# Talking-heads attention and a squared-ReLU FFN: head weights spread by TensorE, later loads, and a last tile in three parts

## The chip, the cores and the metric

The kernel runs on one core of one Trainium2 chip. The metric is the device time of one execution in microseconds. Engines are named as in the profile: PE is TensorE (PEld its weight loads), DVE is VectorE, ACT is ScalarE, POOL is GpSimd, and SP is the engine that issues most DMAs.

## The reference

Eight batches, twelve heads, 448 positions, head dimension 64. Two 12x12 matrices mix the heads, one before and one after the softmax. The result, 3584 rows of 768, goes through a feed-forward network of width 2048.

```python
scores = scale * np.matmul(q, k.transpose(0, 1, 3, 2))       # scale = 1/8
scores = np.einsum('bhij,hg->bgij', scores, w_pre)
scores = scores - np.max(scores, axis=-1, keepdims=True)
attn = np.exp(scores)
attn = attn / (np.sum(attn, axis=-1, keepdims=True) + 1e-09)
attn = np.einsum('bhij,hg->bgij', attn, w_post)
attn_out = np.matmul(attn, v)
x = attn_out.transpose(0, 2, 1, 3).reshape(B * S, H * D)
h = np.maximum(x @ w_in, 0.0)
out = h * h @ w_out
```

All inputs and the output are float32; the matmuls run in bf16.

## The kernel before

**Chunks.** Attention is worked in chunks of ten positions times twelve heads, which are 120 partitions; a batch has 45 chunks, and the run has 360. A chunk `n` goes through a fixed chain. PE mixes the heads of its scores with `wmix` (L775), DVE takes the extreme of each row into `mn` (L786), ACT takes the exponential into `es` with its row sum (L789), DVE takes the reciprocal `rc` (L795), POOL multiplies the head-mixing matrix `wback` by `rc` into `wq` (L798), PE multiplies `es` with `wq` (L805), and DVE or ACT copies that into `atb`. A group of chunks is then multiplied with v (L850) into `xt`, the input of the network.

**Scores.** Scores of 128 positions and one head are computed as 128x448 (L653), copied to `snat` by DVE or ACT, and laid out anew as chunks `sch` by a DMA on SP (L681, a relayout). k and q are transposed before that: in batches 0 and 1 on PE (L509; the last 64 positions of q, the tails, by L549), from batch 2 on by copies `kn<-ks` and `qn<-qs` on POOL or DVE (L584) and a transposing DMA on SP.

**The direct chunks.** In batch 0 the chunks `C0[1] <= c < C0[2]` do not wait for a relayout. For them q is multiplied beforehand with the entries of `w_pre`, on DVE (`f_prep`, L764, into `osb`, used as scratch), and PE forms the mixed scores by six matmuls of 448 columns (L781). The entries stand in `wfan`, which lies in `qn`'s memory and which two DVE operations make from `wall` (L435), a copy of `w_pre` on all partitions. Chunks that are not direct use `wmix` and `wback`, which are made from `wpre_rep`, `wpost_rep` and masks; the direct ones use `wback_far`, made from `wpost_far`.

**The weights of the heads.** Four DMAs on SP bring them, each with a broadcast: `wall` (128 lines of 576 bytes), `wpost_far`, `wpre_rep` and `wpost_rep` (120 lines of 48 bytes each).

**The first loads.** POOL issues k in three pieces (`ks`), q's first 128 positions (in `kn`'s memory), the tails (`qt`) and the rest of q (`qs`), then v and the six pieces of `w_in`. Loads of the next batch are issued on POOL by `load_ahead`, once for heads 0 to 5 and once for heads 6 to 11.

**The network.** Units of 128 or 256 positions: L907 gives `h` (six matmuls per 128 features), DVE or ACT applies the ReLU into `hr` (L921, L925), POOL squares it (L928), and L944 multiplies with `w2` into banks of 384 columns, two per 128 rows. DVE or ACT copies a bank into `osb`, and SP stores it (L968), as 120 rows and 8 rows.

**The order.** A planner (`Planner`) decides the order on every engine when the kernel is built. Each `add` names an engine (or several, with a cost for each), a cost in ns, a priority and what it depends on; the planner plays the run through with these costs and writes down which engine took what when. On the chip each engine then works its list in order. `MOST` limits the banks of each use, `AHEAD` says by how many chunks a relayout goes ahead of its chunk, `gate(n)` holds a load until `wq` of chunk `n`. Where the plan has PE idle early on, it puts in matmuls on zeros (`still`, L1161). The planner's own costs for the first loads and for the preparation on DVE are these:

```python
    set_up = add("DVE", 5300, -100, lambda: None)
...
        at_ += 1.1 if at_ < 2 else 0.75
...
    started = add("POOL", int(1000 * at_) + 700, -100, lambda: None)
```

Of the kernel before, what the change touches and what calls it, by code (L numbers as in the profile page):

```python
# [24 lines left out]
CI = 10  # L25
# [273 lines left out]
def kernel(  # L299
# [124 lines left out]
    def near_back():  # L424
# [4 lines left out]

    smask_far = sb.tile([KC, CI], F32, name="smask_far")  # L430
    nc.vector.tensor_reduce(
        out=smask_far[:, :], in_=ident[0:KC, 0:KC].rearrange("p (h s) -> p s h", h=H), axis=AX.X, op=ALU.add,
    )
    for x in range(2):
        nc.vector.tensor_scalar(  # L435
            out=wfan[64 * x:64 * x + 64],
            in0=wall[64 * x:64 * x + 64, :].rearrange("p (c x g) -> p c x g", x=2, g=H)[:, :, x, :].unsqueeze(3).to_broadcast([D, NPAIR, H, CI]),
            scalar1=-SCALE, scalar2=1.0, op0=ALU.mult, op1=ALU.mult,
        )
    wback_far = sb.tile([KC, H, CI], F32, name="wback_far")  # L440
    nc.gpsimd.tensor_tensor(
        out=wback_far[:, :, :], in0=wpost_far[:, :].unsqueeze(2).to_broadcast([KC, H, CI]),
        in1=smask_far[:, :].unsqueeze(1).to_broadcast([KC, H, CI]), op=ALU.mult,
    )
    qw = [
# [10 lines left out]

    backed = []
    pl = Planner()
# [3 lines left out]
    slots = {}  # L462

    def keep(key, fn):
        def go(*got):
            for key_, slot in zip(key if isinstance(key, list) else [key], got):
                slots[key_] = slot
            fn(*got)
        return go

# [264 lines left out]
    def chunk(b, c):  # L735
# [13 lines left out]
        if far:  # L749
# [4 lines left out]
            for lo, hi, first, x, s0, step, w in (  # L754
                ([(64 * x_, 64 * x_ + 64, 0, zt, P - 8 + x_, 2, 2) for x_ in range(2)] if cc == 0 else []) +
                [(0, P, PIECE * i_, qz[i_], CI * (cc - 1) if cc else P_ROWS - 8, 1, CI if cc else 8) for i_ in range(2)]
            ):
                size = PIECE if lo < hi - 64 else NPAIR
                late = [ready[0, first + y][1][1] for y in range(PIECE)] if size < NPAIR else [ready_tail[0, 0], ready_tail[0, PIECE]]

                def f_prep(eng="DVE", lo=lo, hi=hi, first=first, size=size, x=x, s0=s0, step=step, w=w):
                    o = 2 if w == 8 else 0
                    src_ = x[lo:hi, 0, :, s0:s0 + w] if size < NPAIR else x[lo:hi, :, s0:s0 + step * (w - 1) + 1:step]
                    (nc.vector if eng == "DVE" else nc.gpsimd).tensor_tensor(  # L764
                        out=qw[j][lo:hi, first:first + size, :].rearrange("p c (g s) -> p c g s", g=H)[:, :, :, o:o + w],
                        in0=src_.unsqueeze(2).to_broadcast([hi - lo, size, H, w]),
                        in1=wfan[lo:hi, first:first + size, :, 0:w], op=ALU.mult,
                    )
# [121 lines left out]
    def unit(pair, ui):  # L890
# [47 lines left out]
        for mt in range(w // 128):  # L938
            for nt in range(2):
                key = ("f", ix, "o", mt, nt)  # L940
                for f0 in range(0, FT, 4):
                    def mms(slot, f0=f0, mt=mt, nt=nt):
                        for ft in range(f0, f0 + 4):
                            nc.tensor.matmul(  # L944
                                slot[:, 0:384], lhsT=h2_[:, ft, mt * 128:(mt + 1) * 128],
                                rhs=w2[:, ft, nt * 384:(nt + 1) * 384],
                                start=(ft == 0), stop=(ft == FT - 1),
                            )
                    if f0 == 0:
                        prev = add("PE", 652, fill + 20 + 4 * mt + 2 * nt, keep(key, mms),  # L950
                                   [prev] + sq_op[ix][0:4 // nf] + w2_in[0:1 if ix < SOON else 4], lat=0, bank=key)
                    else:
                        prev = add("PE", 652, FILL, lambda key=key, mms=mms: mms(slots[key]), [prev, w2_in[f0 // 4]] + sq_op[ix][0:(f0 + 4) // nf], lat=0)
# [7 lines left out]
                ev = add({"DVE": 480, "ACT": 440}, 0, 0, evac, [end, st_op.get(si - 2)] + ([m_op[n_] for n_ in direct] if si < 2 else []), lat=100, frees=key)  # L961
                whole = not (z == W2B and mt == 1 and pair == B // 2 - 1)
                evs = evs + [ev] if nt == 1 and whole else [ev]
                if nt == 1 or not whole:
                    done = []
                    for rows, dst, o in pieces(pair, a + mt * 128, None if whole else nt):
                        def store(dst=dst, o=o, rows=rows, si=si, e0=0 if whole else nt * 384, e1=384 if not whole and nt == 0 else DMODEL):
                            nc.sync.dma_start(out=dst, in_=osb[si % 2][o:o + rows, e0:e1])  # L968
                        done.append(add("SP", 510 if rows <= CI else 930, FILL, store, evs))
                    st_op[si] = pl.moved("DMA", 8, 140, 130, 0, done, 1500)  # L970
# [6 lines left out]
    def pieces(pair, pos, part=None):  # L977
        e0, e1 = (0, DMODEL) if part is None else (part * 384, part * 384 + 384)
        got = []
# [25 lines left out]
    def gate(step):  # L1005
        return [wq_op[step]] if step in wq_op else []
# [3 lines left out]

    at_, tails0 = 1.3, []
    for what, x in LOADS0:
        if what == "k":
            k_in[0, x] = first(at_, 28, 48)
        elif what == "q":
            q_in[0, x] = first(at_, 32, 30)
        elif what == "a":
            q_in[0, "a"] = first(at_, 48, 30)
        else:
            tails0.append(first(at_, 24, 24))  # L1020
# [181 lines left out]
```

## Time and profile before

| | |
|---|---|
| median of 3 runs | 585.29 us (584.46 to 587.61) |
| profiled execution | 585.32 us |
| its span | 583.5 us |
| PE busy | 569.2 us (98%), 5813 matmuls |
| DVE busy | 510.9 us (88%) |
| ACT busy | 443.2 us (76%) |
| POOL busy | 321.7 us (55%) |
| granted PE clock | 1.00 |

The span runs from the first to the last instruction that the profile holds. A busy time counts an engine's instructions from start to end; matmuls overlap each other, so PE busy is not PE at its peak. DMA shares are of 16 DMA engines; q0 is the queue that POOL feeds, q1 the one that SP feeds.

### The profile page before, as it was taken

The numbers are of one execution on the slowest core, as the hardware profiler recorded it, in microseconds if no ns is written. First come the engines' busy times: TensorE is split into PE (matmuls) and PEld (weight loads), VectorE is DVE, ScalarE is ACT, GpSimd is POOL, SyncE is SP. The second block draws the span as 40 slices with busy tenths as digits, with TensorE's granted clock in tenths as the row PEclk, the third lists the DMA queues.
The fourth block names the chain that finished last, engine by engine and source line by source line (L and its number), as shares of the span: only waits on it lengthen the run. The fifth ranks groups of instructions, "written<-read, shape, count | busy, mean of one in ns | idle before, by whom it ended". The sixth has DMA issues, their size and how long they took to land.

```text
span 583.5 us, 16716 instructions
## 1 busy us (share of the span) xinstructions
PE 569.2 (98%) x5813; PEld 407.5 (70%) x5813; DVE 510.9 (88%) x1136; ACT 443.2 (76%) x1179; POOL 321.7 (55%) x591
## 2 busy tenths in 40 slices
PE   8999899999999999999999999999999999999996
PEld 5558566777677678667677677767758676767783
DVE  4899998999998999998899998988899998989441
ACT  2688988888797787887887888888788888887200
POOL 7366347646575248735667257734667344635340
PEclk9999999999999999999999999999999999999999
DMA  9999959973797449954596749964397646322021
GB/s 120 213 159 210 185 122 164 205 152 100 143 209 155 125 120 153 188 130 122 102 196 160 163 116 139 197 144 119 95 197 167 155 123 121 116 77 76 2 55 54
DMA packets 132993, 80.98 MB, mean 139 GB/s; under 512 B 60484, under 2 KB 127916, under 8 KB 132908
## 3 DMA queue, kind: packets, MB, share of 16 engines
q1 hardware_dynamic: 85340, 57.11, 38.9%
q0 software_dynamic: 47568, 22.81, 30.7%
q8 instruction: 45, 0.74, 0.5%
q14 instruction: 40, 0.33, 0.2%
HBM read 45.70 MB, written 11.01 MB: 97 GB/s over the span
## 4 chain that ended last, share of the span: by engine, by line
PE 88%; DVE 6%; DMA 3%; issue 1%; ACT 1%; POOL 1%; DVEq 0%; POOLq 0%; ACTq 0%
PE bank L944 25%; PE bank L907 24%; PE bank L805 13%; PE bank L775 11%; PE bank L850 6%; PE bank L653 6%; PE bank L781 2%; DVE mn L786 2%; DMA sch<-snat 2%; DMA ks<-in_k_dram 1%; DVE atb L453 1%; DVE snat L453 1%; PE bank L509 1%; ACT es L789 0%; DVE hr L921 0%
## 5 line engine op out<-in xcount | busy, mean ns | idle before, releaser
L789 ACT ACTIVATE es<-bank,mn 120x448 bf16<-120x448 f32 x360 | 228.7, 641 | 48.4 <-DVE mn L786 44.3
L786 DVE TENSOR_REDUCE mn<-bank 120x1 f32<-120x448 f32 x360 | 209.8, 611 | 4.9 <-PE bank L781 2.9
L798 POOL TENSOR_SCALAR wq<-wback,rc 120x120 bf16<-120x120 f32 (+1 forms) x347 | 122.5, 365 | 157.6 <-DVE rc L795 85.1
L944 PE MATMUL bank<-w,h 128*128 128x384 bf16 x896 | 173.3, 325 | 0.0
L907 PE MATMUL bank<-xt,w 128*128 128x256 bf16 (+1 forms) x1632 | 164.4, 253 | 0.6 <-DVE hr L921 0.4
L928 POOL TENSOR_TENSOR h<-hr 128x512 bf16<-128x512 f32 x112 | 116.3, 1040 | 71.4 <-DVE hr L921 43.7
L907 PEld LDWEIGHTS <-w 128*128 128x128 bf16 x1632 | 136.1, 98 | 25.1 <-issue 4.1
L805 PEld LDWEIGHTS <-es 120*112 120x112 bf16 (+1 forms) x1440 | 107.5, 130 | 30.9 <-ACT es L789 7.0
L453 DVE CAST atb<-bank 112x480 bf16<-112x480 f32 (+2 forms) x197 | 118.5, 610 | 12.1 <-PE bank L805 10.7
L944 PEld LDWEIGHTS <-h 128*128 128x128 bf16 x896 | 84.5, 97 | 55.9 <-issue 2.9
L805 PE MATMUL bank<-wq,es 120*112 120x120 bf16 (+1 forms) x1440 | 118.3, 217 | 3.2 <-POOL wq L798 2.6
L455 ACT CAST atb<-bank 112x480 bf16<-112x480 f32 (+3 forms) x187 | 99.7, 541 | 14.5 <-PE bank L805 13.8
L775 PE MATMUL bank<-sch,wmix 120*128 120x448 bf16 x339 | 105.0, 354 | 1.3 <-DVE snat L453 0.6
L453 DVE CAST snat<-bank 128x448 bf16<-128x448 f32 x152 | 88.2, 612 | 2.6 <-PE bank L653 1.2
L455 ACT CAST snat<-bank 128x448 bf16<-128x448 f32 x172 | 84.8, 544 | 4.9 <-PE bank L653 4.5
L789 ACT ACTIVATION_READ_ACCUMULATOR es<-bank,mn 120x1 f32 x360 | 74.3, 206 | 0.0
L921 DVE TENSOR_SCALAR hr<-bank 128x512 f32<-128x512 f32 x86 | 59.1, 687 | 16.4 <-PE bank L907 14.7
L775 PEld LDWEIGHTS <-wmix 120*128 120x128 bf16 (+1 forms) x347 | 30.7, 98 | 18.5 <-issue 9.7
L850 PE MATMUL bank<-atb,vs 112*64 112x192 bf16 (+3 forms) x864 | 40.4, 250 | 0.3 <-DVE atb L453 0.3
L653 PE MATMUL bank<-kt,qz 64*128 64x448 bf16 x276 | 39.5, 354 | 0.8 <-ACT es L789 0.6
L850 PEld LDWEIGHTS <-vs 112*64 112x64 bf16 x864 | 36.5, 110 | 3.8 <-issue 2.1
L453 DVE COPY osb<-bank 128x384 f32<-128x384 f32 x34 | 18.8, 552 | 17.6 <-PE bank L944 17.2
(63 smaller groups left out, 301.7 us busy)
## 6 DMA issues: line engine op xcount, KB each, us to landing
sch<-snat SPq DMA_DIRECT2D x324, 105.0 KB
out_dram<-osb SPq DMA_DIRECT2D x22, 360.0 KB
vs<-in_v_dram POOLq DMA_DIRECT2D x16, 336.0 KB, 9.1
ks<-in_k_dram POOLq DMA_DIRECT2D x14, 336.0 KB, 8.0
qs<-in_q_dram POOLq DMA_DIRECT2D x14, 288.0 KB, 7.8
w<-in_moe_w_in_dram POOLq DMA_DIRECT2D x6, 512.0 KB, 14.0
w<-in_moe_w_out_dram POOLq DMA_DIRECT2D x4, 768.0 KB, 18.7
out_dram<-osb SPq DMA_DIRECT2D x10, 192.0 KB
```

Of the source, the lines that this page charges most:

```text
L453: nc.vector.tensor_copy(out=out_, in_=in_)
L455: nc.scalar.copy(out=out_, in_=in_)
L653: nc.tensor.matmul(slot[:, 0:S], lhsT=lhsT, rhs=kt[i][half, :, at_, :], start=True, stop=True)
L775: nc.tensor.matmul(slot[:, 0:S], lhsT=wm[0:rows, :], rhs=src[0:rows, :], start=True, stop=True,)
L786: nc.vector.tensor_reduce(out=mn[i][0:rows, :], in_=slots[mk][0:rows, 0:S], axis=AX.X, op=ALU.min)
L789: nc.scalar.activation(out=es[i][0:rows, 0:S], in_=slots[mk][0:rows, 0:S], func=ACT.Exp, scale=-1.0, bias=mn[i][0:rows, 0:1], accum_out=sm ...
L798: nc.gpsimd.tensor_scalar(out=wq[i][0:rows, :, 0:ns], in0=back[0:rows, :, 0:ns], scalar1=rc[i // 2][0:rows, i % 2:i % 2 + 1], scalar2=1.0, ...
L805: nc.tensor.matmul(slot[0:P_KEYS, jb * H * ns:(jb + 1) * H * ns], lhsT=es[i][0:rows, jb * P_KEYS:(jb + 1) * P_KEYS], rhs=wq[i][0:rows, :, ...
L850: nc.tensor.matmul(v_[64 * hh:64 * hh + 64, i, 0:x1 - x0], lhsT=vs[:, 2 * c2 + hh, jb, :], rhs=atb[half][:, jb, 2 * c2 + hh, x0:x1], start ...
L907: nc.tensor.matmul(slot[:, j * w:(j + 1) * w], lhsT=w1[c2][:, (f0 + j) * 128:(f0 + j + 1) * 128], rhs=xt[:, c2, a:z], start=(c2 == 0), sto ...
L928: nc.gpsimd.tensor_tensor(out=h2_[:, f0:f0 + nf, 0:w], in0=hr[gi % 2][:, :].rearrange("p (f c) -> p f c", f=nf), in1=hr[gi % 2][:, :].rear ...
L944: nc.tensor.matmul(slot[:, 0:384], lhsT=h2_[:, ft, mt * 128:(mt + 1) * 128], rhs=w2[:, ft, nt * 384:(nt + 1) * 384], start=(ft == 0), stop ...
```

## The change

The head weights come as two lines on one partition (`row`, 288 numbers). DVE splits each number into three bf16 parts whose sum is the number (`split`), PE multiplies a column of ones with the three parts and adds them in a bank (`spread`), which gives all 288 numbers on all 128 partitions, and ACT copies that to `wall`. `wfan` is made from it as before, but later. `wpre_rep`, `wpost_rep` and `wpost_far`, which take one line of the matrix per partition, are now picked out of `wall` on DVE by a product with a mask and a sum (`pick`). The four broadcast DMAs are gone.

The loads of the next batch take a priority that is two chunks later on POOL (`LATER`), so they go behind `wq` of these chunks where both are ready. `AHEAD` is 7.4 instead of 7.6. The planner's times for the first loads (`FIRST_AT`) and for the preparation on DVE are changed.

The last 128 rows of the output are worked in column parts of 384, 256 and 128 instead of 384 and 384, each copied and stored by itself, and their stores of 8 rows are issued on ACT instead of SP.

As the planner plays the whole run through, the order of instructions changes on every engine from the start on. The numbers of instructions by kind stay the same but for the edits, three more matmuls on PE for `spread`, sixteen more for the third column part, and four `still` fewer (35).

```diff
-AHEAD = 7.6
+AHEAD = 7.4
+LATER = 2
+FIRST_AT = [1.3, 2.4, 3.4, 4.1, 4.9, 5.6, 6.3, 7.0, 7.8]
+FAN_AT, FAR_AT = -14, 1.5
...
-    wall = sb.tile([P, H * H], F32, name="wall")
+    wall = sb.tile([P, 2 * H * H], F32, name="wall")
+    row = sb.tile([1, 2 * H * H], F32, name="row")
+    part = [sb.tile([1, 2 * H * H], BF16, name=f"part{i}") for i in range(3)]
+    one = sb.tile([1, P], BF16, name="one")
+    nc.vector.memset(one[:, :], 1.0)
-    nc.sync.dma_start(out=wall[:, :], in_=w_pre.rearrange("h g -> (h g)").unsqueeze(0).to_broadcast([P, H * H]))
-    nc.sync.dma_start(out=wpost_far[:, :], in_=w_post[:, :].unsqueeze(1).to_broadcast([H, CI, H]))
+    for i, of in enumerate((w_pre, w_post)):
+        nc.sync.dma_start(out=row[:, H * H * i:H * H * (i + 1)], in_=of.rearrange("h g -> (h g)").unsqueeze(0))
...
-    def fetch_weights():
-        nc.sync.dma_start(out=wpre_rep[:, :], in_=w_pre[:, :].unsqueeze(0).to_broadcast([CI, H, H]))
-        nc.sync.dma_start(out=wpost_rep[:, :], in_=w_post[:, :].unsqueeze(0).to_broadcast([CI, H, H]))
+    def split():
+        for i in range(3):
+            nc.vector.tensor_copy(out=part[i][:, :], in_=row[:, :])
+            if i < 2:
+                nc.vector.tensor_tensor(out=row[:, :], in0=row[:, :], in1=part[i][:, :], op=ALU.subtract)
+
+    def spread(slot):
+        for i in range(3):
+            nc.tensor.matmul(slot[:, 0:2 * H * H], lhsT=one[:, :], rhs=part[i][:, :], start=i == 0, stop=i == 2)
+
+    def pick(to, of, mask):
+        parts = hr[0][0:KC, 0:H * H].rearrange("p (g h) -> p g h", g=H)
+        nc.vector.tensor_tensor(
+            out=parts, in0=wall[0:KC, H * H * of:H * H * (of + 1)].rearrange("p (h g) -> p g h", g=H),
+            in1=mask[:, :].unsqueeze(1).to_broadcast([KC, H, H]), op=ALU.mult,
+        )
+        nc.vector.tensor_reduce(out=to[:, :], in_=parts, axis=AX.X, op=ALU.add)
+
+    def pick_near():
+        nc.vector.tensor_reduce(
+            out=own[:, :], in_=ident[0:KC, 0:KC].rearrange("p (s h) -> p h s", s=CI), axis=AX.X, op=ALU.add,
+        )
+        pick(wpre_rep, 0, own)
+        pick(wpost_rep, 1, own)
...
+    def pick_far():
+        nc.vector.tensor_reduce(
+            out=smask_far[:, :], in_=ident[0:KC, 0:KC].rearrange("p (h s) -> p s h", h=H), axis=AX.X, op=ALU.add,
+        )
+        nc.vector.tensor_reduce(
+            out=far_[:, :], in_=ident[0:KC, 0:KC].rearrange("p (h s) -> p h s", h=H), axis=AX.X, op=ALU.add,
+        )
+        pick(wpost_far, 1, far_)
...
-    set_up = add("DVE", 5300, -100, lambda: None)
+    set_up = add("DVE", 1500, -100, lambda: None)
+    in_parts = add("DVE", 1500, -100, split, [set_up, add("FIRST", 0, 0, lambda: None, lat=3300)])
+    walled = add(
+        "ACT", 400, -100, lambda: nc.scalar.copy(out=wall[:, :], in_=slots["m", "wall"][:, 0:2 * H * H]),
+        [add("PE", 200, -100, keep(("m", "wall"), spread), [in_parts], lat=200, bank=("m", "wall"))], frees=("m", "wall"),
+    )
+    fanned = [add("DVE", 720, FAN_AT, lambda x=x: fan(x), [walled]) for x in range(2)]
...
-                got.append(add(PREP[2], 0, n - PREP_AT, f_prep, old + late + [set_up], lat=100))
+                got.append(add(PREP[2], 0, n - PREP_AT, f_prep, old + late + fanned, lat=100))
...
-        w = wq_op[n] = add("POOL", 370, n + 0.5, f_wq, [s_, at_op.get(n - NE)] + (backed if not far else []), lat=70)
...
-            for nt in range(2):
+            whole = not (z == W2B and mt == 1 and pair == B // 2 - 1)
+            cuts = [0, 384, DMODEL] if whole else [0, 384, 640, DMODEL]
+            for nt, (c0, c1) in enumerate(zip(cuts, cuts[1:])):
...
                             nc.tensor.matmul(
-                                slot[:, 0:384], lhsT=h2_[:, ft, mt * 128:(mt + 1) * 128],
-                                rhs=w2[:, ft, nt * 384:(nt + 1) * 384],
+                                slot[:, 0:c1 - c0], lhsT=h2_[:, ft, mt * 128:(mt + 1) * 128],
+                                rhs=w2[:, ft, c0:c1],
                                 start=(ft == 0), stop=(ft == FT - 1),
                             )
...
-                def evac(eng, key=key, si=si, nt=nt):
-                    copy(eng, osb[si % 2][:, nt * 384:(nt + 1) * 384], slots[key][:, 0:384])
+                def evac(eng, key=key, si=si, c0=c0, c1=c1):
+                    copy(eng, osb[si % 2][:, c0:c1], slots[key][:, 0:c1 - c0])
...
-                    for rows, dst, o in pieces(pair, a + mt * 128, None if whole else nt):
-                        def store(dst=dst, o=o, rows=rows, si=si, e0=0 if whole else nt * 384, e1=384 if not whole and nt == 0 else DMODEL):
-                            nc.sync.dma_start(out=dst, in_=osb[si % 2][o:o + rows, e0:e1])
-                        done.append(add("SP", 510 if rows <= CI else 930, FILL, store, evs))
+                    for rows, dst, o in pieces(pair, a + mt * 128, None if whole else (c0, c1)):
+                        side_ = not whole and rows <= CI
+                        def store(dst=dst, o=o, rows=rows, si=si, e0=0 if whole else c0, e1=DMODEL if whole else c1, eng=nc.scalar if side_ else nc.sync):
+                            eng.dma_start(out=dst, in_=osb[si % 2][o:o + rows, e0:e1])
+                        done.append(add("ACT" if side_ else "SP", 510 if rows <= CI else 930, FILL, store, evs))
...
-    at_, tails0 = 1.3, []
-        at_ += 1.1 if at_ < 2 else 0.75
+    tails0 = []
+    for what, us in zip(LOADS0, FIRST_AT):
...
-    started = add("POOL", int(1000 * at_) + 700, -100, lambda: None)
+    started = add("POOL", int(1000 * FIRST_AT[-1]) + 1400, -100, lambda: None)
...
-    fetched = add("SP", 1700, NEAR_AT, fetch_weights, [k_in[0, 2]], lat=2500)
+    picked = add("DVE", 1000, FAR_AT, pick_far, [walled])
+    backed_far.append(add("POOL", 420, FAR_AT, far_back, [picked]))
+    fetched = add("DVE", 900, NEAR_AT, pick_near, [walled, k_in[0, 2]])
...
-            load(48, (36, 52), n, lambda: load_q(b, g0, g0 + 6), wars + gate(n)),
-            load(42, (46, 58), n, lambda: load_kv(ks, k, b, g0, g0 + 6), wars + gate(n)),
...
-            load_tails(b, n, got_tail[b - 1] + gate(n))
+            load_tails(b, n + LATER, got_tail[b - 1] + gate(n))
```

More of the change, by code (lines that the diff above doesn't have):

```diff
@@ new lines, in pick_near, with fan @@
+    def pick_near():
[4 more added lines that the diff above has]
+        pick(wpost_rep, 1, own)
+    def fan(x):
+        nc.vector.tensor_scalar(
+            out=wfan[64 * x:64 * x + 64],
+            in0=wall[64 * x:64 * x + 64, 0:H * H].rearrange("p (c x g) -> p c x g", x=2, g=H)[:, :, x, :].unsqueeze(3).to_broadcast([D, NPAIR, H, CI]),
+            scalar1=-SCALE, scalar2=1.0, op0=ALU.mult, op1=ALU.mult,
+        )
@@ new lines, in pick_far, with far_back @@
+    def pick_far():
[6 more added lines that the diff above has]
+        pick(wpost_far, 1, far_)
+    def far_back():
+        nc.gpsimd.tensor_tensor(
+            out=wback_far[:, :, :], in0=wpost_far[:, :].unsqueeze(2).to_broadcast([KC, H, CI]),
+            in1=smask_far[:, :].unsqueeze(1).to_broadcast([KC, H, CI]), op=ALU.mult,
+        )
@@ L428, in near_back @@
         )
[L430 to L444, printed above, removed]
     qw = [
@@ L832, in chunk @@
             e.next.append(s_)
-        w = wq_op[n] = add("POOL", 370, n + 0.5, f_wq, [s_, at_op.get(n - NE)] + (backed if not far else []), lat=70)
+        w = wq_op[n] = add("POOL", 370, n + 0.5, f_wq, [s_, at_op.get(n - NE)] + (backed_far if far else backed), lat=70)
         old = [op for half in {u[0] for u in where} for op in av_op[b - 1, half]] if b > 0 else []
@@ L956, in unit @@
                 si = ix_store[0]
-                def evac(eng, key=key, si=si, nt=nt):
-                    copy(eng, osb[si % 2][:, nt * 384:(nt + 1) * 384], slots[key][:, 0:384])
-                ev = add({"DVE": 480, "ACT": 440}, 0, 0, evac, [end, st_op.get(si - 2)] + ([m_op[n_] for n_ in direct] if si < 2 else []), lat=100, frees=key)
-                whole = not (z == W2B and mt == 1 and pair == B // 2 - 1)
+                def evac(eng, key=key, si=si, c0=c0, c1=c1):
+                    copy(eng, osb[si % 2][:, c0:c1], slots[key][:, 0:c1 - c0])
+                ev = add({"DVE": 80 + (c1 - c0) * 25 // 24, "ACT": 165 + (c1 - c0) * 5 // 7}, 0, 0, evac, [end, st_op.get(si - 2)] + ([m_op[n_] for n_ in direct] if si < 2 else []), lat=100, frees=key)
                 evs = evs + [ev] if nt == 1 and whole else [ev]
@@ L1009, in first @@
         return pl.moved("LOAD", rows, each, each, 0, [add("FIRST", 0, us, lambda: None, lat=1000 * us + 1600)], 1300)
-    at_, tails0 = 1.3, []
[L1012 to L1020, printed above, removed]
-        at_ += 1.1 if at_ < 2 else 0.75
+    tails0 = []
+    for what, us in zip(LOADS0, FIRST_AT):
+        if what[0] == "k":
+            k_in[0, what[1]] = first(us, 28, 48)
+        elif what[0] == "a":
+            q_in[0, "a"] = first(us, 48, 30)
+        elif what[0] == "q":
+            q_in[0, what[1]] = first(us, 32, 30)
+        elif what[0] == "t":
+            tails0.append(first(us, 24, 24))
     tail_in[0] = add("TAIL", 0, 0, lambda: None, tails0, lat=0)
-    started = add("POOL", int(1000 * at_) + 700, -100, lambda: None)
+    started = add("POOL", int(1000 * FIRST_AT[-1]) + 1400, -100, lambda: None)
     def w_turn(slot):
```

29 lines of the change are left out of this document (18 added, 11 removed).

## Prediction

> **What bounds the kernel now.** I read the page's busy rows first, then the busy time by stretches, then the timeline of both ends.
>
> ```profile
> PE 569.2 (98%) x5813; PEld 407.5 (70%) x5813; DVE 510.9 (88%) x1136; ACT 443.2 (76%) x1179; POOL 321.7 (55%) x591
> ```
>
> PE (matmul) is the bound on average. The stretches (start:end, length, then busy us and instructions of PE, PEld, DVE, ACT, POOL, granted clock, DMA share, GB/s) tell where it isn't:
>
> ```profile
> 0.00:5.00 5.00, 3.94 (x19) 2.75 (x20) 1.76 (x7) 1.28 (x1) 3.81 (x11) 1.00 0.31 36
> 5.00:10.00 5.00, 3.79 (x36) 2.19 (x34) 1.55 (x6) 0.00 (x0) 4.19 (x7) 1.00 1.31 146
> ...
> 40.00:60.00 20.00, 19.44 (x344) 15.05 (x343) 19.37 (x48) 18.27 (x52) 13.95 (x24) 1.00 1.27 205
> 60.00:80.00 20.00, 18.02 (x245) 12.21 (x242) 19.70 (x47) 17.33 (x48) 7.74 (x19) 1.00 0.86 171
> ...
> 100.00:550.00 450.00, 447.88 (x4545) 324.89 (x4543) 415.17 (x904) 367.48 (x980) 256.27 (x477) 1.00 0.68 139
> ...
> 579.00:583.50 4.50, 0.00 (x0) 0.00 (x0) 0.51 (x1) 0.00 (x0) 0.00 (x0) 1.00 0.19 60
> ```
>
> From 100 to 550 us PE idles 2.1 us in 450: there no edit to another engine pays. What can move is the load-bound start (DMA share above 1 from 5 us on), the stage from 20 to 100 us, where PE idles 4.9 us (18.71, 19.44, 18.02 and 18.90 busy in its four stretches of 20) while DVE is busy 19.4 and 19.7 of 20, and the last 4.5 us, which are one copy and a store.
>
> The start by the timeline (start, us, what; in brackets the idle time before and who ended it):
>
> ```profile
> 3.80 1.47 DVE L435 TENSOR_SCALAR qn<-wall 64x720 bf16<-64x720 f32 x2 [2.36 <-DMA wall<-in_w_pre_dram]
> ...
> 10.99 0.96 PE L509 MATMUL bank<-ident,ks 112*64 112x112 bf16 x16 [0.39 <-DMA ks<-in_k_dram]
> ...
> 13.73 2.45 PE L781 MATMUL bank<-kt,osb 128*120 128x448 bf16 x6
> ...
> 17.84 1.30 PE L781 MATMUL bank<-kt,osb 128*120 128x448 bf16 x6
> ```
>
> PE waits for k's second piece until 10.99 and then runs without a break. The same six matmuls take 2.24 us in the chain of waits the first time and 1.14 the second: PE runs at half rate until about 17.1 us, though the granted clock reads 1.00.
>
> The end:
>
> ```profile
> 578.95 0.56 DVE L453 COPY osb<-bank 128x384 f32<-128x384 f32 x1 [2.04 <-PE bank L944]
> ```
>
> ```profile
> 579.54 1.29 SPq L968 DMA_DIRECT2D out_dram<-osb  x2
> ```
>
> After the last matmul come the 384-column copy, 0.79 us to issue the 120-row store and 0.50 for the 8-row one; by the DMA view their data moves from 580.95 to 581.95, and the span ends at 583.5.
>
> The profiled execution took 585.32 us for a span of 583.5 (1.8 outside it); the median of the three runs is 585.29, so one sum serves both.
>
> **The last tile in three parts.** PE: 16 matmuls of 384 columns become 16 of 256 and 16 of 128. Matmuls of 128 columns with a weight load each run at 56 ns (24 L907 in 1.34 in the chain), of 256 at 109 (96 in 10.48), of 384 at 163 (64 in 10.41): 56 + 109 = 165 for 163, nothing. The last copy has 128 columns instead of 384: 448 columns take 0.61 and 384 take 0.55, which gives 0.31 by slope, 0.25 less. The 8-row store moves to ACT, which is idle at the end (no busy time after 550 us), so it no longer stands behind 0.79 us of SP. Before, the last data ended 2.4 us after the first issue began; now it should end at 1.4 (issue to first data, 579.54 to 580.95) plus a third of 180 KB (579.54's 180 KB and its small one took 1.0), say 0.35: 0.65 less. What comes after the data stays. Sum -0.9; bounds -0.25 (the copy alone, the store no quicker) and -1.2 (the small store entirely off the path).
>
> [...]
>
> **w_pre and w_post as single lines.** Removed: four broadcast DMAs on SP.
>
> ```profile
> q0 software_dynamic: 4855, 1.55, 103.3%
> q1 hardware_dynamic: 536, 0.09, 5.1%
> ```
>
> This is the DMA view over 0 to 14 us (packets, MB, share of 16 engines). Of q1's 0.71 us, 7.4% of 5 to 6, 9.7% of 6 to 8 and 1.7% of 8 to 10, together 0.30 us, lie where the loads saturate the engines; the rest runs beside unsaturated time. So k's later pieces land 0.3 earlier, and PE's run begins at 10.7. Bounds 0 (the loads are held by POOL's issues) and -0.7. I take -0.3.
>
> Added on PE: three matmuls of 288 columns, 0.24 us each at the rate of the standing ones (256 in 0.213), in time that `still` matmuls fill. On ACT one copy, 0.4, in idle time (ACT's first work is at 10.64). On DVE the split: five operations on 1x288; nearest rows are 128x360 bf16 (0.28) and 128x448 from a bank (0.61); I take 0.35 each, 1.75. The far picks: one reduce (0.37), one product (0.27 as L418), one reduce (0.3): 0.94. The near picks: one reduce and two such pairs, 1.5. Total 4.2 us, bounds 3.4 and 6.
>
> What hides them: DVE idles 5.6 us between 5.7 and the first max at 16.22. But the chain now starts later. The line lands about when `wall` did (3.8; two issues, small data; bounds 3.3 and 4.3), split to 5.55, matmuls and ACT copy to about 7.2, then the fan (1.47) that had been done at 5.3. From 7.2, DVE has 4.9 us of old work, 1.47 fan, 0.37, 0.94 and 1.5 picks and 0.46 of `wmix` (it stood at 24.4): 9.6, so 16.8 instead of 16.22, less the 0.38 of `kt` that the order of the instructions gives to ACT. The order also puts four tail scores ahead of the first direct chunk on PE (1.5 us at half rate), so PE has work while DVE is late. I take +0.3. Bounds 0 and +2.5 (all of the upper DVE cost, landing at 4.3, nothing hidden): DVE is full afterwards, so what is late here stays late to 100 us.
>
> **Loads behind wq** (LATER), AHEAD. Each `load_ahead` issues q (0.87), k (0.78) and once two tail DMAs (1.32) on POOL. It is moved past up to two wq per batch (0.35 each).
>
> ```profile
> PE bank L805 <- POOL wq L798: 2.6, 4, 1.1
> ```
>
> PE waited for wq four times in the run, and where I looked the wq had waited for DVE's rc, not for a load (39.15: 0.25 idle on POOL, ended by rc). Gain 0, bounds -1.0 and the stall of the rival below. AHEAD moves relayouts 0.2 chunk later: 0.
>
> **The new order from 20 to 100 us.** The planner deals every copy anew: by the order of instructions DVE loses 9 `atb` and 9 `hr` copies and gains 12 `snat`; PE's turns of mode go from 178 to 180. Work is the same; what can change is the 4.9 us of PE idle there. The tails' `snat` come before the first direct chunk, so the relayouts that the chain waits for at 55 (7.6 us of DMA sch) start earlier. I take -0.5; bounds -3 and +3.
>
> Sum: -0.9 - 0.3 + 0.3 - 0.5 = -1.4: 585.32 - 1.4 = 583.9.
>
> **Rivals.** (a) The new order closes most of the idle time from 20 to 100: -3 in place of -0.5, 581.4. For it: DVE is at 97% there and gives nine large copies to ACT, which had 1.7 to 4.4 us free in each 20. Against: DVE gets twelve others.
>
> (b) PE reaches full rate sooner. A run of standing matmuls of 4.7 us (1.06 to 5.74) did not raise it, one of 6.1 (10.99 to 17.1) did, so the onset can lie 1.4 us earlier, which is worth half, 0.7; if the early run sufficed, all after the last load (13.1) is at full rate, (17.1 - 13.1) / 2 = 2.0. I price it 1.6: 582.3. [...]
>
> (c) Slower: a k load too late. By the order, the second k load of batch 2 goes from behind the 52nd wq to behind the 62nd, and its first cast (`kn<-ks`) stands behind the 70th wq on POOL and the 71st max on DVE. The 52nd to 94th wq took 57 us (95.5 to 152.9), 1.36 each: 8 chunks are 10.9 us, and a load of this kind lands in 8.0:
>
> ```profile
> ks<-in_k_dram POOLq DMA_DIRECT2D x14, 336.0 KB, 8.0
> ```
>
> It decides from a landing of 10.9 us. Behind the waiting casts stand wq on POOL and max on DVE, and PE runs dry. Other loads take 14.0 and 18.7 us: 3 to 8 late, say 5: 588.9. Against: no other large load runs beside it.
>
> (d) The change does nothing beyond its tail, 584.4.
>
> **How the numbers follow.** The forecast 0.42, (a) 0.24, (b) 0.13, (c) 0.13, (d) 0.08. A difference under 0.5% (2.9 us: 582.4 to 588.2) is about what a measurement of this kernel can tell from no change. Faster is (a) and (b), 0.37; within is the forecast and (d), 0.50; slower is (c), 0.13. The range reaches down to (a) with the tail's upper bound, 580.8, and up to the forecast with DVE's upper bound and half the order's, 583.9 + 2.2 + 1.5 = 587.6; (c) is left out.
>
> **What would show it.** Right: k's second transposes at about 10.7; the first max at 16.5 to 17; last copy 0.3 us, and from the last matmul's end to the span's end 3.6 us instead of 4.6; PE idle from 20 to 100 between 3 and 5 us. Wrong: PE idle there under 2.5 (a); six L781 matmuls in 1.3 us before 16 (b); a `kn` cast that waits for ks near 110 us (c); a store on ACT that lands last.

## The result, and the profile after

The changed kernel takes 582.32 us (median of 12 runs, 581.79 to 584.79); the kernel before took 585.18 us beside it (12 runs, 584.14 to 587.61). The ratio is 0.9956 with a 95% interval of 0.9942 to 0.9969. That is 2.6 us less by the ratio: inside the band of 0.5%, but clear of no change. The profiled execution took 582.16 us for a span of 580.4.

Busy times of the page after (us, share of the span, instructions):

```profile
PE 566.6 (98%) x5828; PEld 405.5 (70%) x5828; DVE 510.2 (88%) x1144; ACT 447.6 (77%) x1188; POOL 321.2 (55%) x590
```

PE's busy time fell by 2.6 us though it has 15 matmuls more; idle time fell only from 14.3 (583.5 - 569.2) to 13.8. The same stretches as before (start:end, length, busy us and instructions of PE, PEld, DVE, ACT, POOL, granted clock, DMA share, GB/s), kernel after:

```profile
0.00:5.00 5.00, 3.94 (x20) 2.59 (x20) 2.65 (x11) 1.28 (x1) 3.80 (x11) 1.00 0.44 52
5.00:10.00 5.00, 3.92 (x81) 2.63 (x79) 4.23 (x13) 2.60 (x7) 5.00 (x7) 1.00 1.60 168
...
40.00:60.00 20.00, 19.43 (x344) 14.92 (x339) 19.06 (x48) 18.61 (x52) 11.80 (x21) 1.00 1.28 216
60.00:80.00 20.00, 18.67 (x257) 13.53 (x256) 19.58 (x44) 17.04 (x46) 9.10 (x18) 1.00 0.59 127
...
100.00:550.00 450.00, 447.19 (x4526) 323.16 (x4524) 408.54 (x894) 368.34 (x978) 255.05 (x474) 1.00 0.70 139
```

The row to read is the second one. PE ran 81 matmuls from 5 to 10 us where it had run 36, in the same busy time. With the other rows of that span PE idles 4.3 us from 20 to 100 (4.9 before), and 2.8 from 100 to 550 (2.1 before). So the gain isn't idle time closed in the middle; it is work that starts sooner and, in this execution, runs at PE's full rate (called full and half rate here: in the timelines the same six direct matmuls take 1.30 to 1.35 us or 2.1 to 2.45).

The start by the timeline of the kernel after (start, us, what, idle time before and who ended it):

```profile
2.47 0.30 DVE L414 CAST part<-row 1x288 bf16<-1x288 f32 x1 [0.89 <-DMA row<-in_w_post_dram]
...
4.65 0.54 PE L420 MATMUL bank<-part,one 1*128 1x288 bf16 x3
5.22 0.40 ACT L525 COPY wall<-bank 128x288 f32<-128x288 f32 x1 [3.20 <-PE bank L420]
5.66 0.53 DVE L438 TENSOR_SCALAR qn<-wall 64x720 bf16<-64x720 f32 x1 [1.10 <-ACT wall L525]
...
8.50 0.58 PE L555 MATMUL bank<-ident,ks 112*64 112x112 bf16 x16 [0.25 <-DMA ks<-in_k_dram]
...
12.21 0.73 PE L827 MATMUL bank<-kt,osb 128*120 128x448 bf16 x3
...
14.34 1.35 PE L827 MATMUL bank<-kt,osb 128*120 128x448 bf16 x6
```

The two lines land at 2.47, not at 3.8, and `wall` is whole at 5.62. k's second transposes start at 8.50 instead of 10.99 and take 0.58 instead of 0.96. The first six direct matmuls (three and three) run at the full rate from 12.21; before they ran at half of it from 13.73. k's first transposes, at 5.55, take 0.58 us already (0.96 at 6.57 before).

Why k is early stands in the DMA view over 0 to 14 us (packets, MB, share; then KB each and median us from issue to landing), kernel after:

```profile
q0 software_dynamic: 5277, 1.74, 114.4%
...
q1 hardware_dynamic: 4, 0.00, 0.0%
...
ks<-in_k_dram POOLq DMA_DIRECT2D x3, 224.0 KB, 5.0
```

The same row of the kernel before:

```profile
ks<-in_k_dram POOLq DMA_DIRECT2D x3, 224.0 KB, 7.5
```

POOL issues the first of these loads at 1.32 us after and 1.31 before, the next at 3.49 and 3.48: same issues, landings 2.5 us sooner by the median of the three. The rows of q say the same (7.1 to 4.8, 7.3 to 4.3).

The end, timeline after:

```profile
574.43 3.26 SPq L1016 DMA_DIRECT2D out_dram<-osb  x3
574.44 2.66 ACTq L1016 DMA_DIRECT2D out_dram<-osb  x3
...
576.49 0.29 DVE L493 COPY osb<-bank 128x128 f32<-128x128 f32 x1 [0.47 <-PE bank L992]
```

From the start of the last copy to the end of the span it is 3.91 us (580.4 - 576.49); before it was 4.55. From the last matmul's end it is 3.94 us, before 4.63, and 3.6 was forecast.

### The profile page after: what moved, and what is told of

It reads as the page before. It is cut to its first block, busy times and chain, and to the rows that moved or that the text cites. A ratio compares the mean times of both kernels' runs of the same rounds, so it can differ in the third digit from the quotient of the medians.

```text
span 580.4 us, 16784 instructions
## 1 busy us (share of the span) xinstructions
PE 566.6 (98%) x5828; PEld 405.5 (70%) x5828; DVE 510.2 (88%) x1144; ACT 447.6 (77%) x1188; POOL 321.2 (55%) x590
## 4 chain that ended last, share of the span: by engine, by line
PE 84%; DVE 9%; DMA 2%; ACT 2%; issue 2%; POOL 1%; SPq 0%; DVEq 0%; POOLq 0%; ACTq 0%
PE bank L992 24%; PE bank L953 23%; PE bank L851 12%; PE bank L821 10%; PE bank L896 7%; PE bank L699 6%; DMA sch<-snat 2%; DVE mn L832 2%; DVE atb L493 2%; DVE snat L493 1%; ACT es L835 1%; DVE osb L810 1%; PE bank L1210 1%; POOL wq L844 0%; ACT snat L495 0%
## 5 line engine op out<-in xcount | busy, mean ns | idle before, releaser
L992 PE MATMUL bank<-w,h 128*128 128x384 bf16 (+2 forms) x912 | 173.4, 323 | 0.0
L953 PE MATMUL bank<-xt,w 128*128 128x256 bf16 (+1 forms) x1632 | 164.2, 254 | 0.2
L953 PEld LDWEIGHTS <-w 128*128 128x128 bf16 x1632 | 136.0, 98 | 26.2 <-issue 5.4
L992 PEld LDWEIGHTS <-h 128*128 128x128 bf16 x912 | 85.9, 97 | 58.4 <-issue 4.1
L851 PEld LDWEIGHTS <-es 120*112 120x112 bf16 (+1 forms) x1440 | 105.0, 130 | 28.5 <-issue 5.8
L493 DVE CAST atb<-bank 112x480 bf16<-112x480 f32 (+3 forms) x186 | 111.8, 609 | 11.4 <-PE bank L851 10.4
L495 ACT CAST atb<-bank 112x480 bf16<-112x480 f32 (+3 forms) x198 | 105.4, 542 | 17.0 <-PE bank L851 15.8
L851 PE MATMUL bank<-wq,es 120*112 120x120 bf16 (+1 forms) x1440 | 115.8, 217 | 2.2 <-POOL wq L844 1.4
L493 DVE CAST snat<-bank 128x448 bf16<-128x448 f32 x164 | 95.4, 611 | 4.0 <-PE bank L699 1.9
L495 ACT CAST snat<-bank 128x448 bf16<-128x448 f32 x160 | 79.2, 544 | 3.2 <-PE bank L699 3.1
L967 DVE TENSOR_SCALAR hr<-bank 128x512 f32<-128x512 f32 x77 | 52.9, 688 | 15.3 <-PE bank L953 12.2
L493 DVE COPY osb<-bank 128x384 f32<-128x384 f32 (+2 forms) x36 | 19.4, 540 | 18.2 <-PE bank L992 18.1
```

The costliest lines, as they stand in the source:

```text
L493: nc.vector.tensor_copy(out=out_, in_=in_)
L495: nc.scalar.copy(out=out_, in_=in_)
L851: nc.tensor.matmul(slot[0:P_KEYS, jb * H * ns:(jb + 1) * H * ns], lhsT=es[i][0:rows, jb * P_KEYS:(jb + 1) * P_KEYS], rhs=wq[i][0:rows, :, ...
L953: nc.tensor.matmul(slot[:, j * w:(j + 1) * w], lhsT=w1[c2][:, (f0 + j) * 128:(f0 + j + 1) * 128], rhs=xt[:, c2, a:z], start=(c2 == 0), sto ...
L992: nc.tensor.matmul(slot[:, 0:c1 - c0], lhsT=h2_[:, ft, mt * 128:(mt + 1) * 128], rhs=w2[:, ft, c0:c1], start=(ft == 0), stop=(ft == FT - 1),)
```

## The experiments

Each was timed in 12 runs (one in 11) beside the kernel before. A ratio below 1 is faster than before; 0.001 is 0.59 us. What is read in a profile is one execution of the 12.

**e1, the kernel before without the four broadcasts.** The weights are constants here, so the head mixing is another one; the order is that of before.

```diff
-    nc.sync.dma_start(out=wall[:, :], in_=w_pre....to_broadcast([P, H * H]))
-    nc.sync.dma_start(out=wpost_far[:, :], in_=w_post....to_broadcast([H, CI, H]))
+    nc.vector.memset(wall[:, :], 0.1)
+    nc.vector.memset(wpost_far[:, :], 0.1)
...
     def fetch_weights():
-        nc.sync.dma_start(out=wpre_rep[:, :], ...)
-        nc.sync.dma_start(out=wpost_rep[:, :], ...)
```

> The kernel before with its own order of instructions; the four broadcast loads of the head weights are left out and the four tiles filled with a constant, so the output isn't the reference's. Theory A (the broadcasts hold up the first loads): k's second transposes come at about 8.5 us instead of 10.99 and the time falls by 1.5 to 2.5 us, to about 583. Theory B (what the change gained is PE's early full rate, luck of the profiled runs): the loads may land earlier but the time falls by less than 0.7 us. The prediction's own term was 0.3 us.

Measured: 0.9967 (0.9953 to 0.9981), 1.9 us less. In its DMA view:

```profile
ks<-in_k_dram POOLq DMA_DIRECT2D x3, 224.0 KB, 5.1
```

By the median of its three pieces k lands as soon as in the changed kernel, and the time falls as theory A had it, by most of the gain of the whole change. The piece that PE waits for came later than that: k's second transposes start at 9.68 in this profile, 1.3 us sooner than before, not at the 8.5 that was expected; POOL issued that piece 0.5 us later here (3.96 instead of 3.48). The rest of the difference to 8.50 is not explained.

**e2, only the three loads of 48-byte lines left out,** `wall` kept.

```diff
-    nc.sync.dma_start(out=wpost_far[:, :], in_=w_post....to_broadcast([H, CI, H]))
+    nc.vector.memset(wpost_far[:, :], 0.1)
...
     def fetch_weights():
-        nc.sync.dma_start(out=wpre_rep[:, :], ...)
-        nc.sync.dma_start(out=wpost_rep[:, :], ...)
```

> As the kernel without the broadcasts, but wall (128 lines of 576 bytes) is still loaded; only the three loads of 120 lines of 48 bytes are left out, their tiles filled with a constant (output not the reference's). Theory A1 (the 48-byte lines do the harm): nearly all of the gain of the kernel without any broadcast, k's second transposes before 9 us. Theory A2 (it is the broadcast of 72 KB): little of it, k's second transposes after 10 us, time within 0.5 us of before.

Measured: 0.9963 (0.9947 to 0.998), 2.1 us less, as much as e1. So 17 KB in 360 lines cost the time, and the 72 KB of `wall` in 128 lines add nothing to it that can be measured, though they do hold the loads: the median landing of k is 6.4 us here, between 7.5 before and 5.1 in e1. Its timeline:

```profile
9.92 0.95 PE L510 MATMUL bank<-ident,ks 112*64 112x112 bf16 x16 [1.45 <-DMA ks<-in_k_dram]
...
12.66 2.45 PE L782 MATMUL bank<-kt,osb 128*120 128x448 bf16 x6
```

k's second transposes are 1.1 us sooner, which misses the sign of theory A1 (before 9 us) though the time came as A1 had it. PE is at half rate in this execution, which took 585.25, 1.7 above the median of its own runs.

**e3, ten more standing matmuls (`still`, on zeros) before the first direct chunk,** in the order of before.

```diff
+EXTRA = {22: 4, 28: 4, 29: 2}
...
+        for _ in range(1 + EXTRA.get(n_still[0], 0)):
             nc.tensor.matmul(...)
```

> The kernel before with ten more matmuls on zeros, placed where PE idled at 5.7, 8.7 and 10.0 us, so that PE is kept busy from 1.06 to 10.5 us. Theory B (the rate of PE at the start decides): the six L781 matmuls of the first direct chunk take 1.2 us instead of 2.24, and the time falls by 1.5 to 2.0 us, to about 583.5. Theory A: the matmuls are quicker, but DVE and the loads set the pace, and the time falls by less than 0.7 us.

Measured: 0.9988 (0.9972 to 1.0003), not told apart from no change. The rate went up early (k's transposes at 11.35 took 0.58) and fell again:

```profile
14.02 2.09 PE L782 MATMUL bank<-kt,osb 128*120 128x448 bf16 x6
```

The granted clock shows the fall: it reads 0.50 from 12.2 to 15.6, behind a stretch (8.8 to 12.2) in which PE was busy 1.81 us of 3.40. So in this execution the edit didn't bring about the full rate whose worth it was to measure. Some of its other runs differ in this; what they say stands under rival (b) below.

**e4, the tail alone,** on the kernel before: the diff's last part (the cuts at 384 and 640, the 8-row stores on ACT).

```diff
-            for nt in range(2):
+            whole = not (z == W2B and mt == 1 and pair == B // 2 - 1)
+            cuts = [0, 384, DMODEL] if whole else [0, 384, 640, DMODEL]
+            for nt, (c0, c1) in enumerate(zip(cuts, cuts[1:])):
...
```

> The kernel before with the last tile in three column parts and its 8-row stores on ACT, nothing else; the order is the same up to the last tile. The prediction's term is -0.9 us (bounds -0.25 and -1.2); the two profiles of before and after give 4.55 and 3.91 us from the last copy's start to the span's end, which with the column parts is -0.6 us. [...] Expected 584.4 to 584.7; a store on ACT that lands last would make it 585 or more.

Measured: 0.998 (0.9968 to 0.9991), 1.1 us less. Last copy to end: 582.5 - 579.06 = 3.44.

**e5, all but the tail and the two numbers of the order.**

```diff
-AHEAD = 7.4
+AHEAD = 7.6
-LATER = 2
+LATER = 0
...
-            cuts = [0, 384, DMODEL] if whole else [0, 384, 640, DMODEL]
+            cuts = [0, 384, DMODEL]
...
-                        side_ = not whole and rows <= CI
+                        side_ = False
```

> The kernel after without LATER (0), with AHEAD at 7.6 and with the last tile as before: only the head weights by PE and the planner's new times for the start. Theory A (the loads): most of the gain, -1.8 to -2.5 us, about 583. If the gain came from the later loads or from a lucky order: within 0.7 us of before.

Measured: 1.0024 (1.001 to 1.0039), 1.4 us slower than before, which neither expectation held, though k's second transposes start at 8.94. The early start was there and was lost later. The edit also sets one planner's cost back (ACT's copy of an output bank, 440 ns instead of 439).

**e6, the changed kernel with `LATER = 0`.**

```diff
-LATER = 2
+LATER = 0
```

> The kernel after with LATER at 0, everything else as after. The prediction gave this part nothing: within 0.5 us of after (582.3). If putting the loads behind wq pays, it is 583 or more; if the late k load costs, it is below 582.

Measured: 1.0061 (1.0039 to 1.0083), 3.6 us slower than before and some 6 slower than the changed kernel. The stretches of e6 where it loses:

```profile
120.00:130.00 10.00, 8.25 (x69) 4.86 (x66) 9.55 (x23) 9.38 (x28) 3.18 (x10) 1.00 0.79 149
130.00:140.00 10.00, 8.49 (x52) 4.83 (x52) 7.12 (x16) 5.94 (x16) 3.15 (x7) 0.66 0.60 151
```

and the same ones of the kernel after:

```profile
120.00:130.00 10.00, 10.00 (x98) 8.33 (x96) 9.94 (x24) 8.15 (x23) 6.29 (x11) 1.00 0.64 159
130.00:140.00 10.00, 10.00 (x91) 6.84 (x89) 9.71 (x20) 7.56 (x21) 6.18 (x10) 1.00 0.45 132
```

In e6 the network's first matmuls (L953) are missing until 133 us: 4.4 us of them from 110 to 140 against 11.8 in the kernel after, where 9.0 lie between 121 and 133. PE idles 3.3 us from 120 to 140. The granted clock falls to 0.66 in the second stretch, which costs again: an estimated 3.4 us of PE's work, (1 - 0.66) times 10. No load is late: e6 issues the next batch's from 86 to 94 us, the kernel after from 86 to 91 and at 106. It reads as if the planner had used up too early the network's work that fills PE between chunks, which was not tested further. The 0.66 comes with the idle stretch; that the idle time brings it was not tested.

**e7, the changed kernel with the 8-row stores on SP.**

```diff
-                        side_ = not whole and rows <= CI
+                        side_ = False
```

> The kernel after with the 8-row stores of the last tile on SP again, everything else as after. If ACT as second issuer saves the issue of the last small store, it is 0.5 us slower than after, about 582.8; if the fixed time of the store sets the end, equal to after.

Measured: 0.9968 (0.9953 to 0.9983). The stores on ACT are worth 0.7 us by the two ratios, whose intervals overlap; by the spans, last copy to end is 4.3 us (581.7 - 577.38) against 3.91. On every engine but for these stores the instructions and their order are those of the changed kernel.

**e8, the picks on PE.** The lines are multiplied with a 0/1 matrix on PE instead of picked on DVE; the planner orders anew.

```diff
-        nc.vector.tensor_reduce(out=to[:, :], in_=parts, axis=AX.X, op=ALU.add)
...
+        for i in range(3):
+            nc.tensor.matmul(slot[0:KC, 144:168], lhsT=hot[:, 0, :], rhs=lpart[i][:, :], start=i == 0, stop=i == 2)
...
```

> The kernel after with the picks on PE: w_pre and w_post also come as 12 lines of 48 bytes, DVE splits 12x24 numbers, and six small matmuls with a 0/1 matrix give wpre_rep, wpost_rep and wpost_far, so the two far and near picks of DVE (2.7 us of products and sums) are gone; the planner orders it anew. Theory C (DVE is the bound of the start once the loads are early: 4.8 and 4.9 of 5 us busy from 10 to 20 us): 0.5 to 2 us faster than after, 580.3 to 581.8. Theory A alone (loads set the start): equal to after within 0.5 us.

Measured: 0.998 (0.9957 to 1.0002), neither faster than the changed kernel (theory C) nor shown equal to it; its runs spread from 580.28 to 588.21. DVE is no less busy from 10 to 15 us (4.86 against 4.83).

**e9, the changed kernel with `AHEAD = 7.6`.**

```diff
-AHEAD = 7.4
+AHEAD = 7.6
```

> The kernel after with AHEAD at 7.6 (LATER stays 2). It fills the square of AHEAD 7.4 or 7.6 and LATER 0 or 2: so far 7.4 with 2 is after (582.3), 7.4 with 0 gave 589.3, 7.6 with 0 (with the old last tile, 1.1 us more by the tail's run) 586.4, so about 585.3 with the new one. Theory L (the loads behind wq pay by themselves): 7.6 with 2 is 2 us or more below 585.3, so 583 or less, and the effect of LATER has the same sign at both values. Theory P (each value gives another order, and the order as a whole is good or bad): no common effect; 7.6 with 2 may as well be 585 to 588.

Measured: 1.0004 (0.9992 to 1.0016), the whole gain gone, so theory L fell. With e6 and e5 that makes a square, whose last cell is only near: e5 has the old tail and the planner's cost named there, and so an order of its own.

| | LATER 2 | LATER 0 |
|---|---|---|
| AHEAD 7.4 | 0.9956 | 1.0061 |
| AHEAD 7.6 | 1.0004 | 1.0024 without the new tail, 1.0004 by e4's 0.0020 for it |

`LATER` is worth 6 us at 7.4 and, as far as the last cell goes, nothing at 7.6, so neither number has a price of its own: they choose among orders. One stretch of e9 where its order is worse:

```profile
160.00:250.00 90.00, 87.19 (x884) 62.00 (x884) 84.60 (x187) 73.67 (x199) 55.31 (x103) 1.00 0.86 156
```

and of the kernel after:

```profile
160.00:250.00 90.00, 88.49 (x914) 63.16 (x911) 85.13 (x192) 77.66 (x208) 56.34 (x104) 1.00 0.95 157
```

PE idles 2.8 us there instead of 1.5 (2.7 in e5, where the granted clock also falls to half once more, for 3.4 us at 236).

**e10, the kernel before with `LATER = 2`.**

```diff
-            load(48, (36, 52), n, lambda: load_q(b, g0, g0 + 6), wars + gate(n)),
+            load(48, (36, 52), n + LATER, lambda: load_q(b, g0, g0 + 6), wars + gate(n)),
...
```

> The kernel before with the loads of the next batch two chunks later in priority (LATER 2), nothing else; the planner orders it anew from 36 us on. Theory L: 2 us or more faster than before. Theory P: anything from -3 to +3 us, without a reason in the waits for loads.

Measured: 1.0012 (0.9992 to 1.0033, 11 runs). This run can't decide between the theories. By the traces every engine has the same instructions in the same order as in the kernel before, the loads on POOL too: `LATER` moves nothing there, and the same program was timed twice. The ratio shows how far two such timings differ (0.7 us).

**e11, an attempt at a version that beats both:** the order of before, the three small loads issued behind the first loads at 10.5 to 12.4 us, the new tail, nine more standing matmuls. `wback_far` is made later on POOL than before, since its weights come later.

```diff
     def fetch_weights():
+        pass
+
+    def fetch_late():
+        nc.sync.dma_start(out=wpost_far[:, :], ...)
         nc.sync.dma_start(out=wpre_rep[:, :], ...)
...
     def near_masks():
+        fetch_late()
```

> The kernel before in its own order, with three edits that the runs point to: the three loads of 48-byte lines are issued only at about 12 us, when the masks are made (a memset of their tiles holds them), the last tile is in three parts, and nine more matmuls on zeros stand at the start. Nothing is left out of the computation. By the runs so far: -2.1 (small loads) - 1.1 (tail) - 0.4 (rate of PE), so 581.8; at or a little below after (582.3). If the loads do the same harm later (they meet v and w_in then), it is 583.5 or more.

Measured: 1.004 (1.0024 to 1.0056), 2.3 us slower than before. Its timeline says why:

```profile
12.44 0.76 SPq L408 DMA_DIRECT2D wpost_rep<-in_w_post_dram  x1
...
21.09 0.39 POOL L432 TENSOR_TENSOR wback<-wpost_rep,smask 120x120 f32<-120x120 f32 x1 [6.34 <-DMA wpost_rep<-in_w_post_dram]
...
23.22 0.90 PE L818 MATMUL bank<-wq,es 120*112 120x120 bf16 x8 [3.79 <-POOL wq L811]
```

5.6 KB took 8.6 us beside the large loads. `wback` waits for it at the head of POOL's list, `wback_far` and every `wq` stand behind it, and PE runs dry for 3.8 us. Up to then this kernel was 2.8 us ahead of before (the first max ended at 14.0 against 16.8).

**e12, the changed kernel without the picks,** in its own order; the small weights are constants here.

```diff
     def pick(to, of, mask):
-        ...
+        pass
```

> The kernel after in its own order, with the eight operations of the picks left out on DVE (the products with masks and the sums, 2.7 us) and their three tiles filled with a constant, so the output isn't the reference's. Theory C (DVE's added work in the start costs time): 0.7 to 2 us faster than after, 580.3 to 581.6. The prediction's term (+0.3 us): within 0.5 us of after.

Measured: 0.9968 (0.9952 to 0.9984), the same as the changed kernel within the intervals: the picks on DVE cost nothing that can be measured, which leaves room for about 1 us. Its profiled execution took 585.82, 2.85 above its own median, with PE at half rate:

```profile
14.75 2.23 PE L818 MATMUL bank<-kt,osb 128*120 128x448 bf16 x6
```

## Why the prediction was right, and where its sum was wrong

The forecast was 583.9 and within 0.5%; measured were 582.32 and a ratio inside that band. The sum came near for partly wrong reasons: the loads were mis-sized by 1.6 to 1.8 us, what is left for the new order came out on the other side, and that the two nearly cancel is luck.

- **The loads (-0.3): mis-sized; measured -1.9 (e1) and -2.1 (e2).** This is the step that failed. The prediction took the time of the SP queue's packets in the saturated stretch, 0.30 us, as what they took from the others, and had k's second transposes at 10.7. They start at 8.50 in the changed kernel: beside the broadcasts the loads landed 2.5 us later, with the same issue times. Why so few packets hold the others up for so long no run shows. A part of the 1.9 and 2.1 goes with PE's rate, as rival (b) below has it. The bound of -0.7 was the whole packet time of that queue, and so was no bound. Leaving out the three loads of 48-byte lines brings the whole 2.1 us (e2), but the landings of k (6.4 with `wall` kept, 5.1 without) say that the 576-byte lines of `wall` hold others too, and e2 doesn't tell the size of the lines from their number.
- **The tail (-0.9): right, -1.1 (e4).** The copy took 0.29 (0.31 worked out), and from the last matmul's end to the span's end it is 3.53 us in e4 (3.6 forecast). The profile of the changed kernel has 3.94 for the same tail; why is not shown. e4's interval (-0.5 to -1.9) doesn't tell the 0.9 from 0.75, which is the copy's 0.25 and the 0.50 that SP took to issue the 8-row store before.
- **DVE's new work (+0.3): not seen.** The split took 2.08 us (2.47 to 4.55, 1.75 worked out), but it started at 2.47 instead of 3.8, and the first max came at 15.39 where 16.5 to 17 was forecast (16.22 before). With all picks gone (e12) the time is the same within about 1 us, so a term of 0.3 is not refuted either.
- **`LATER` by itself (0): not tested by itself.** In the kernel before it moves nothing (e10). In the changed kernel the order comes with it: without it the time is 6 us longer (e6).
- **The new order (-0.5): it is what is left, -2.6 + 1.9 + 1.1 = +0.4.** PE's idle time from 20 to 100 fell by 0.6, as forecast, and rose by 0.7 from 100 to 550, where the prediction held that nothing would move. The three intervals, some 0.7 to 0.8 us to either side each, leave the sign of this remainder open. That it is so small was luck: by the same subtraction the neighbouring orders cost +3.3 (e5: 1.4 + 1.9), +3.2 (e9: 0.2 + 1.9 + 1.1) and +6.6 (e6: 3.6 + 1.9 + 1.1), if the parts add. The bound of +3 was too narrow, and AHEAD "0.2 chunk later: 0" was wrong at `LATER` 2 (2.8 us between the kernel after and e9).

**The rivals.** (a) fell: PE still idles 4.3 us from 20 to 100. (c) didn't happen. The second k load of batch 2 is issued at 106.37, and its cast on POOL found the data there, as no idle time stands before it:

```profile
117.69 0.61 POOL L630 COPY kn<-ks 112x512 bf16<-112x512 bf16 x1
```

(d) fell: the loads bring more than the tail.

(b) did better than the forecast. Its price, 582.3, is the time that was measured, and the sign that the prediction gave for it came nearly so: the first six direct matmuls of the profiled execution take 0.73 and 0.78 us before 16 (1.3 in all was the sign). One execution doesn't show that the change does it. That of e7, with the same order, falls back to half rate at 11.4:

```profile
8.00:11.40 3.40, 2.07 (x50) 1.56 (x50) 3.23 (x13) 2.32 (x6) 3.04 (x5) 1.00 1.85 175
11.40:14.80 3.40, 3.40 (x13) 1.79 (x14) 3.33 (x12) 1.97 (x5) 3.40 (x6) 0.50 1.33 164
...
13.18 2.11 PE L827 MATMUL bank<-kt,osb 128*120 128x448 bf16 x6
```

But the mean granted clock of every run is on record. A fall to half for 3.4 us, as here, makes it 0.997 over the run, and one for 6.8 us, as in e4 and e10 from about 9 to 16, makes it 0.994. Of 35 runs of the kernel before (those beside e9 to e12) 27 read 0.992 to 0.995; of the 12 of the changed kernel none does, three read 0.996 or 0.997 and nine 0.999 or 1.000 (e7: none, eight and four). The mean doesn't say when the clock fell; in the profiles of e1 to e4, e7 and e10 it fell between 9 and 17 us, and e5, e6 and e11 have a later fall. So PE seems to keep its rate at the start more often after the change. What goes with that can be read where runs of one kernel differ (mean us, number of runs in brackets, before as timed beside e1 to e4):

| mean granted clock | 0.992 to 0.995 | 0.996 to 0.998 | 0.999 or 1.000 |
|---|---|---|---|
| before | 585.8 (25) | 584.9 (6) | 585.7 (4) |
| e1 | 584.6 (6) | 583.3 (4) | 582.7 (2) |
| e2 | 585.1 (3) | 583.3 (7) | 582.0 (2) |
| e3 | 586.5 (3) | 585.5 (6) | 583.7 (3) |

In e1 to e3 a run without a fall is 1.9 to 3.1 us shorter than one with about 6.8 us of it; (b) was priced at 1.6, an estimate between its 0.7 and 2.0. A reading of 1.000 has two meanings, though: in the trace of the kernel before the first clock record lies at 17.1 us (at 4.4 after), and the time ahead of it counts as 1.00. So that profiled execution reads 1.000 though it ran at half rate until 17.1 (the six in 2.24 us), and some runs of the last column may be like it. At an equal clock (the first two columns) e1 and e2 are 0.7 to 1.6 us shorter than before; the rest of their gain goes with the rate. This is an association, not a cause shown: no run here sets the rate, and the effects of the rate and of the earlier loads were not separated.

**Slips in the working.** (a) with the tail's upper bound is 581.1 and not 580.8, and half the order's bound, counted from the -0.5 in the sum, gives 588.1 and not 587.6. DVE is at 97% from 40 to 80 us and at 94% from 20 to 100; it loses 11 `atb` copies, not nine (197 before, 186 after). Nothing above depends on these.

**What stays open:** what makes the order at 7.4 and 2 better than its three neighbours. The places where the others lose are shown (120 to 140 in e6, 160 to 250 in e5 and e9), the planner's decision that leads there is not. Open too is how much of the gain runs through PE's rate, and why small packets delay the large loads by so much more than their own time.

## What to carry to other kernels

Price a small DMA beside saturated loads by when the others land, not by its own packets' time: three loads of 5.6 KB in 48-byte lines cost 2 us here, and picking the same data out on the chip cost nothing that could be measured (e12). Where a planner orders the whole run, an edit has no price of its own; run its neighbours in the planner's settings too, since a gain at the start can be kept (0.9956) or given back (1.0004 to 1.0061) a hundred microseconds later. A load that is put off so as not to disturb others can itself become the one that everything waits for (8.6 us for 5.6 KB, and PE dry for 3.8, in e11). Look whether an edit changes the program at all before its time is read (e10), and read the granted clock of all runs, not only of the one that was profiled.

## What the runs showed of the hardware that was not expected

- Four broadcasts on one queue, 0.30 us of the engines' time where the loads saturate them, held up the first loads on the other queue by 2.5 us (medians: 7.5 against 5.0 and, in e1, 5.1). Without the 360 lines of 48 bytes it was 1.1 less (6.4), and the kernel gained as much as without all four (e2 2.1 us, e1 1.9).
- A load of 5.6 KB, issued at 12.44 beside the large ones, was there only at 21.09.
- PE's rate in the first 17 us differs between executions of the same order (0.73 and 0.78 us for the first six direct matmuls after, 2.11 in e7). The granted clock shows a fall (0.50 from 11.4 to 14.8 in e7), but not the half rate ahead of its first record (17.1 us in the trace of the kernel before): the rows of that kernel read 1.00 while the six take 2.24 us.
- Runs of one kernel whose mean granted clock is 0.992 to 0.995 were 1.9 to 3.1 us longer than those at 0.999 or 1.000 (e1, e2, e3).
